# A written order for the first feed-forward block, a third raw buffer, and first attention tiles taken from three batches

## The chip, the cores and the metric

The kernel runs on one core of a Trainium2 chip. Its engines are TensorE (PE in the rows; PEld is its weight load), VectorE (DVE), ScalarE (ACT), GpSimd (POOL) and SyncE (SP, which only issues transfers here); 16 DMA engines move the data. The metric is device time in microseconds (us) of one execution, the median of several; lower is better.

## The reference

Three stages in a row, with 3072 tokens (4 batches of 768), 8 heads of 40, a model width of 320 and a hidden width of 2048.

```python
# attention: an mLSTM recurrence over t, per batch and head
m_new  = max(f[t] + m, i[t]);  f_stab = exp(f[t] + m - m_new);  i_stab = exp(i[t] - m_new)
C      = f_stab * C + i_stab * outer(v[t], k[t]);   n = f_stab * n + i_stab * k[t]
y[t]   = sigmoid(o[t]) * (C @ q[t]) / max(|n . q[t]|, 1)
# first feed-forward layer
h = maximum(x @ w_in, 0);  x = (h * h) @ w_out
# second feed-forward layer
h = x @ w2_in;  x = (h * sigmoid(h)) @ w2_out
```

## The kernel before, in words

**Gates.** The recurrence is computed in 24 tiles of 128 tokens, six chunks c for each batch b. `gate_math` runs two scans over all 768 steps on 32 partitions (batch times head) on VectorE, which give `gg` (a log weight) and `eg` (its exponent). Both are written to DRAM (`g_d`, `e_d`) so that transfers can read them back spread over 128 partitions. `gate_T` transposes two more rows into `aw`.

**An attention tile** i goes through small functions: `load_q` and `load_v` (tiles `kq`, `vk`), `load_w` (512 KB of `g_d` spread into `W`), `WT` (GpSimd masks `W`), `WE` (eight exponents on ScalarE), `SC` (scores, TensorE into `sc`), `SD` (VectorE, scores times `W`), `HG` (TensorE into `hA`: the tile's own part, and for c > 0 the earlier chunks' part from the state `cm`), `EV` (VectorE: division and output gate `sg`, into `y`), `ST`, `GR` (the new state), `XT`, `XA`, `XL` (transpose `y` and split it into a high and a low part in `x`). For c > 0, `QT` scales q by `eq`, which `load_e` reads back from `e_d`. The first six tiles use float32 matmuls, each of which the trace shows as two.

**The first layer** works on eight blocks of 384 tokens (three tiles). Hidden slice j of 16 takes eight matmuls into `hin` ("in j"), a Relu and two squares on ScalarE (`r`, `gh`, `r` again), a subtraction on VectorE (`gl`), and eight matmuls into `o` ("out j"). TensorE is three slices ahead with "in" (`AHEAD`). The second layer has six blocks of 512 tokens.

**Weights** arrive as 64-bit numbers, in 16 pieces per layer (eight "in", eight "out"). Each piece is loaded into a `raw` buffer (two of them), turned into float32 by one ScalarE (L171) and two VectorE instructions (L173, L174; tile `dt`), and split: ScalarE writes the high part (L185, L197), GpSimd the low one (L188, L189, L200 for the first layer). The first seven or so pieces are decoded before the first block begins, the others during it; the second layer's pieces follow during blocks 1 to 6 and go back to DRAM.

**Order.** Up to the first block a scheduler orders the engines, guided by the order of the code. From there TensorE's order is that of the code; in blocks 1 to 6 that of ScalarE, VectorE and SP too. Attention tiles 3 to 23 are spread over the blocks by `base` and `plan`. The first three tiles are (batch 0, chunk 0), (batch 1, chunk 0) and (batch 0, chunk 1), by

```python
TILES = [(b, c) for p in (0, 2) for c in range(NC) for b in (p, p + 1)]
```

Of the kernel before, what the change touches and what calls it, by code (L numbers as in the profile page):

```python
# [22 lines left out]
L = 128  # L23
# [8 lines left out]
EC = 1  # L32
W_BUFS = 2
N_NAT = 6
W_U0 = 4
# [4 lines left out]
G_PAT = "a"  # L40
W_LA = 4
TILES = [(b, c) for p in (0, 2) for c in range(NC) for b in (p, p + 1)]
# [19 lines left out]
def mlstm_moe_kernel(  # L62
# [39 lines left out]
    ident = const.tile([128, 128], F32, name="ident")  # L102
    bmask = const.tile([128, 9, 1], F32, name="bmask")
# [7 lines left out]
    gg = gp.tile([32, S], F32, name="gg")  # L111

# [4 lines left out]
    def consts():  # L117
        pool.memset(eg, 1.0)
        pool.memset(eg.rearrange("p (c t) -> p c t", t=L)[:, :, 0:1], 0.0)
        make_identity(nc, ident)  # L120
        pool.memset(bmask, 1.0)
# [7 lines left out]
    def gate_math():  # L129
        dve.tensor_tensor_scan(out=w_r, data0=fg, data1=a_r, initial=NEG, op0=ALU.add, op1=ALU.max)  # L130
        dve.tensor_tensor(out=fg[:, 1:S], in0=fg[:, 1:S], in1=w_r[:, 0:S - 1], op=ALU.add)
        dve.tensor_tensor(out=fg[:, 1:S], in0=fg[:, 1:S], in1=w_r[:, 1:S], op=ALU.subtract)
        dve.memset(fg[:, 0:1], 0.0)
        dve.tensor_tensor_scan(out=gg, data0=eg, data1=fg, initial=0.0, op0=ALU.mult, op1=ALU.add)
        act.activation(out=eg, in_=gg, func=ACTF.Exp)
        dve.tensor_tensor(out=a_r, in0=a_r, in1=w_r, op=ALU.subtract)
        dve.tensor_tensor(out=a_r, in0=a_r, in1=gg, op=ALU.subtract)
        g3 = gg.rearrange("p (c t) -> p c t", t=L)
        dve.tensor_tensor(out=w_r.rearrange("p (c t) -> p c t", t=L),
                          in0=a_r.rearrange("p (c t) -> p c t", t=L),  # L140
                          in1=g3[:, :, L - 1:L].to_broadcast([32, NC, L]), op=ALU.add)
        act.activation(out=w_r, in_=w_r, func=ACTF.Exp)
        sp.dma_start(out=g_d, in_=gg)
        sp.dma_start(out=e_d, in_=eg)

    def gate_T():
        ps = p_at.tile([128, 512], F32, tag="at", name="gT")
        pv = ps[:, 0:2 * NC * 32].rearrange("p (a c r) -> p a c r", a=2, r=32)
        for k, src in enumerate((a_r, w_r)):
            for c in range(NC):  # L150
                pe.transpose(pv[:, k, c, :], src[:, c * L:(c + 1) * L], ident[0:32, 0:32])
        dve.tensor_copy(out=aw, in_=pv)
# [4 lines left out]
    def w_in_load(w, u, pl):  # L157
        st = pl.tile([128, 3, 256, 2], I32, tag="raw", name="raw")
        sp.dma_start(out=st, in_=w[u].bitcast(I32).rearrange("p (k f two) -> p k f two", k=3, two=2))
        return st.rearrange("p k f two -> p (k f) two")  # L160

    def w_out_load(w, u, pl):
        st = pl.tile([128, 768, 2], I32, tag="raw", name="raw")[:, 0:640]
        sp.dma_start(out=st, in_=w[u].bitcast(I32).rearrange("p (n two) -> p n two", two=2))
        return st

    def w_split(raw, which, layer, u, pl):
        n = 768 if which == "i" else 640
        lo, hi = raw[:, :, 0], raw[:, :, 1]
        t = pl.tile([128, 768], I32, tag="dt", name="dt")[:, 0:n]  # L170
# [6 lines left out]
        if which == "i":  # L177
# [3 lines left out]
            else:  # L181
                ws = pl.tile([128, 1280], F32R, tag="raw", name="ws")
# [4 lines left out]
            eng = pool if layer == 1 else dve  # L187
            eng.tensor_tensor(out=w[:, 3:5], in0=tv[:, 0:2], in1=f(w[:, 0:2]), op=ALU.subtract)  # L188
            eng.tensor_tensor(out=w[64:128, 2], in0=tv[64:128, 2], in1=f(w[64:128, 2]), op=ALU.subtract)  # L189
        elif layer == 1:  # L190
# [8 lines left out]
            for c, oh, ol in parts:  # L199
                pool.tensor_tensor(out=w[:, :, ol], in0=tv[:, :, c], in1=f(w[:, :, oh]), op=ALU.subtract)  # L200
        else:
            ws = pl.tile([128, 1280], F32R, tag="raw", name="ws")
# [18 lines left out]

    eq = [at.tile([128, 3, EC * L], F32, name=f"eq{k}") for k in range(2)]
    cc2 = [at.tile([128, H, 42], F32, name=f"cc{k}") for k in range(2)]
    T = {}

    def at_consts():
        for k in range(2):
            pool.memset(eq[k][:, 2, :], 0.0)
            pool.memset(cc2[k], 0.0)

    def load_q(i):
        b, c = TILES[i]
# [12 lines left out]
    def load_v(i):  # L245
        v = T[i]["vk"] = at.tile([128, DM + 2 * VW], F32, tag="vk", name="vk", bufs=2)
# [15 lines left out]
    def load_w(i):  # L262
        b, c = TILES[i]
        d = T[i]
        w = at.tile([128, H, L], F32, tag="W", name="W", bufs=W_BUFS)
        d["W", 0], d["W", 1] = w[:, 0:4], w[:, 4:8]
        sp.dma_start(out=w, in_=g_d[b * H:(b + 1) * H, c * L:(c + 1) * L].unsqueeze(0).to_broadcast([128, H, L]))

    def load_e(i):
        b, c = TILES[i]  # L270
        if c % EC == 0 and c + EC > 1:
            for g in range(3):
                n = min(3, H - 3 * g)
                h = b * H + 3 * g
                sp.dma_start(out=eq[b % 2][0:40 * n, g, :],
# [556 lines left out]
```

## Time and profile before

| | |
|---|---|
| median of 3 runs | 872.77 us (871.34 to 873.82) |
| profiled execution | 871.93 us, its span 869.9 us |
| TensorE busy | 832.7 us, 96% of the span |
| weight loads busy | 784.0 us, 90% |
| VectorE, ScalarE | 493.1 and 495.5 us, 57% each |
| GpSimd | 97.3 us, 11% |
| transfers | 117.41 MB, 135 GB/s over the span |

The span runs from the first to the last instruction. Matmuls are pipelined, so each one's time in the trace is longer than the distance to the next; the pace of TensorE is read from start to start. An average over the span hides that the stages have different limits, so most views below are of single stretches.

### The profile page before, as it was taken

The numbers are of one execution on the slowest core, as the hardware profiler recorded it, in microseconds if no ns is written. First come the engines' busy times: TensorE is split into PE (matmuls) and PEld (weight loads), VectorE is DVE, ScalarE is ACT, GpSimd is POOL, SyncE is SP. The second block draws the span as 40 slices with busy tenths as digits, with TensorE's granted clock in tenths as the row PEclk, the third lists the DMA queues.
The fourth block names the chain that finished last, engine by engine and source line by source line (L and its number), as shares of the span: only waits on it lengthen the run. The fifth ranks groups of instructions, "written<-read, shape, count | busy, mean of one in ns | idle before, by whom it ended". The sixth has DMA issues, their size and how long they took to land.

```text
span 869.9 us, 14594 instructions
## 1 busy us (share of the span) xinstructions
PE 832.7 (96%) x5492; PEld 784.0 (90%) x5492; DVE 493.1 (57%) x879; ACT 495.5 (57%) x969; POOL 97.3 (11%) x119
## 2 busy tenths in 40 slices
PE   4768989999999999999999999999999999999998
PEld 3758989999999999999999899999999999999997
DVE  5466756777778778787852234353343443533432
ACT  4567846787797777977855563343343433433332
POOL 4574500000101000100000010000000000000000
PEclk9999999999999999999999999999999999999999
DMA  8786455767767768768510894020020000000000
GB/s 241 236 277 188 130 165 181 237 212 220 234 212 228 245 189 246 234 218 255 171 57 31 256 293 153 1 80 1 1 79 1 1 31 1 31 1 1 31 0 31
DMA packets 71391, 117.41 MB, mean 135 GB/s; under 512 B 5146, under 2 KB 50138, under 8 KB 71082
## 3 DMA queue, kind: packets, MB, share of 16 engines
q1 hardware_dynamic: 71322, 116.49, 43.0%
q8 instruction: 43, 0.70, 0.3%
q14 instruction: 26, 0.21, 0.1%
HBM read 77.23 MB, written 19.33 MB: 111 GB/s over the span
## 4 chain that ended last, share of the span: by engine, by line
PE 76%; DMA 8%; DVE 5%; ACT 5%; SPq 2%; issue 2%; POOL 1%; DVEq 0%; ACTq 0%; POOLq 0%
PE hin L539 36%; PE o L594 6%; PE o L593 6%; PE o L592 6%; PE o L575 4%; PE o L577 4%; PE o L576 4%; DMA eq<-e_d 3%; PE hA L406 2%; PE o L580 2%; PE o L582 2%; DMA raw<-in_w_in_dram 2%; DMA sg<-in_og_dram 1%; PE sc L331 1%; PE hA L396 1%
## 5 line engine op out<-in xcount | busy, mean ns | idle before, releaser
L539 PE MATMUL hin<-x,wi 128*128 128x384 f32 (+1 forms) x1792 | 401.9, 366 | 7.7 <-ACT r L547 4.5
L539 PEld LDWEIGHTS hin<-x,wi 128*128 128x128 f32 x1792 | 324.2, 190 | 36.4 <-ACT r L547 5.8
L559 DVE TENSOR_TENSOR gl<-r,gh 128x384 fp32r<-128x384 f32 (+1 forms) x224 | 142.7, 639 | 113.8 <-ACT gh L556 60.7
L555 DVE TENSOR_TENSOR r<-hin,r 128x512 f32<-128x512 f32 x96 | 66.4, 691 | 136.4 <-ACT r L554 136.4
L554 ACT ACTIVATE r<-hin 128x512 f32<-128x512 f32 x96 | 57.3, 597 | 148.2 <-PE hin L539 148.2
L594 PE MATMUL o<-wo,gl 128*128 128x320 f32 x384 | 118.7, 309 | 0.0
L593 PE MATMUL o<-wo,gh 128*128 128x320 f32 x384 | 118.5, 309 | 0.0
L592 PE MATMUL o<-wo,gh 128*128 128x320 f32 x384 | 118.2, 308 | 0.0
L547 ACT ACTIVATE r<-hin 128x384 f32<-128x384 f32 x128 | 62.3, 486 | 79.2 <-PE hin L539 72.4
L556 ACT ACTIVATE gh<-r 128x512 fp32r<-128x512 f32 x96 | 60.6, 632 | 65.4 <-DVE r L555 65.4
L575 PE MATMUL o<-gh,wo 128*128 128x384 f32 x256 | 90.2, 352 | 0.0
L577 PE MATMUL o<-gl,wo 128*128 128x384 f32 x256 | 86.7, 339 | 0.0
L576 PE MATMUL o<-gh,wo 128*128 128x384 f32 x256 | 86.6, 338 | 0.0
L592 PEld LDWEIGHTS o<-wo,gh 128*128 128x128 f32 x384 | 72.1, 188 | 3.6
L593 PEld LDWEIGHTS o<-wo,gh 128*128 128x128 f32 x384 | 72.1, 188 | 3.6
L308 POOL TENSOR_SCALAR_AFFINE_SELECT W<-W 128x512 f32<-128x512 f32 x48 | 39.2, 841 | 301.1 <-DMA W<-g_d 189.6
L594 PEld LDWEIGHTS o<-wo,gl 128*128 128x128 f32 x384 | 72.1, 188 | 0.0
L316 ACT ACTIVATE W<-W,aw 128x128 f32<-128x128 f32 x192 | 59.9, 388 | 16.8 <-POOL W L308 16.7
L548 ACT ACTIVATE gh<-r 128x384 fp32r<-128x384 f32 x128 | 67.2, 525 | 3.8
L550 ACT ACTIVATE r<-r 128x384 f32<-128x384 f32 x128 | 67.0, 524 | 3.7
L575 PEld LDWEIGHTS o<-gh,wo 128*128 128x128 f32 x256 | 48.5, 189 | 0.5
L576 PEld LDWEIGHTS o<-gh,wo 128*128 128x128 f32 x256 | 48.5, 189 | 0.1
(108 smaller groups left out, 1060.1 us busy)
## 6 DMA issues: line engine op xcount, KB each, us to landing
stk<-tt SPq DMA_DIRECT2D x162, 120.0 KB
raw<-in_w_in_dram SPq DMA_DIRECT2D x16, 768.0 KB
W<-g_d SPq DMA_DIRECT2D x24, 512.0 KB
raw<-in_w_out_dram SPq DMA_DIRECT2D x16, 640.0 KB
vk<-in_vk_dram SPq DMA_DIRECT2D x24, 328.0 KB
rqk<-in_qk_dram SPq DMA_DIRECT2D x18, 360.0 KB
w2i_d<-ws SPq DMA_DIRECT2D x8, 640.0 KB
w2o_d<-ws SPq DMA_DIRECT2D x8, 640.0 KB
```

Source lines behind the costliest of these rows:

```text
L539: pe.matmul(ps[:, 0:N], w[:, c, ws], x[:, sl, 0:N], start=(k == 0), stop=(k == 7))
L547: act.activation(out=r, in_=ps[:, 0:N], func=ACTF.Relu)
L548: act.activation(out=gh, in_=r, func=ACTF.Square)
L550: act.activation(out=g, in_=r, func=ACTF.Square)
L555: dve.tensor_tensor(out=g, in0=ps[:, 0:N], in1=r, op=ALU.mult)
L559: low.append(lambda: on("gl" if ly == 1 else "gl2", gi).tensor_tensor(out=gl, in0=g, in1=f(gh), op=ALU.subtract))
L575: pe.matmul(o[k][:, 0:N], w[:, c], gh, start=first, stop=False)
L576: pe.matmul(o[k][:, 0:N], w[:, c2], gh, start=False, stop=False)
L577: pe.matmul(o[k][:, 0:N], w[:, c], gl, start=False, stop=last)
L592: pe.matmul(o[k][:, 0:DM], gh[:, c], w[:, 0:320], start=first, stop=False)
L593: pe.matmul(o[k][:, 0:DM], gh[:, c], w[:, 320:640], start=False, stop=False)
L594: pe.matmul(o[k][:, 0:DM], gl[:, c], w[:, 0:320], start=False, stop=last)
```

## The change

Everything up to the end of the first block is no longer left to a scheduler. Each step gets a name, a planned time from a table (`ORDER`) and a list of steps that must stand ahead of it; all are sorted by that time and written out in that order on all five engines. Besides:

- the first three tiles are chunk 0 of batches 0, 1 and 2 (so none of them reads `cm` or `eq`), and batch 3 comes last, its six chunks one behind the other;
- the gate scans are cut into chunk 0 and the other five chunks; `g_d` of chunk 0 and `W` of tiles 0 to 2 are issued from ScalarE's queue;
- there are three `raw` buffers for two; "in" pieces are loaded ahead of "out" pieces (i0, i1, o0, i2, ...);
- the scores of the first six tiles have four heads on partitions 0 to 39 and four on 64 to 103, in turn;
- in the first block some squares move from ScalarE to VectorE, the low parts of pieces i1, i7, o3, o4 and o6 from GpSimd to VectorE;
- 21 filler matmuls of 512 columns on zeros (`warm`) stand between the first ones, two of them behind the start of the block.

```diff
+GA = L
+RAW_BUFS = 3
+DT_BUFS = 2
-TILES = [(b, c) for p in (0, 2) for c in range(NC) for b in (p, p + 1)]
+WARM = ((4, "o0"), (5, "o0"), (2, "in"), (3, "in"), (3, "in"), (2, "in"), (2, "in"))
+ORDER = """
+    gates 0 ee0 0 sg:0 0.05 q:0 0.1 q:1 0.2 c1 0.26 v:0 0.3 c0 0.39 c2 0.4 v:1 0.5 warm0 0.98 gD0 1.24 wz 1.62
...
+PLAN = {k: float(v) for k, v in zip(ORDER.split()[0::2], ORDER.split()[1::2])}
...
+TILES = [(b, c) for c in range(NC) for b in range(3)] + [(3, c) for c in range(NC)]
...
+            lambda: (act if first else sp).dma_start(out=g_d[:, c], in_=gg[:, c]),
+            lambda: sp.dma_start(out=e_d[:, c], in_=eg[:, c]),
...
+    def warm(n, tag="o2"):
+        ps = (p_in if tag == "in" else p_out).tile([128, 512], F32, tag=tag, name="warm")
+        for _ in range(n):
+            pe.matmul(ps.rearrange("p (h t) -> p h t", h=4), wz, wz.unsqueeze(1).to_broadcast([128, 4, L]),
+                      start=True, stop=True)
...
-            eng = pool if layer == 1 else dve
+            eng = pool if layer == 1 and PLAN.get(f"@Mi{u}", 1) else dve
...
+        q, m = (act, 4) if i < N_EARLY else (sp, H)
+        for p in range(0, H, m):
+            q.dma_start(out=w[:, p:p + m], in_=g_d[b * H + p:b * H + p + m, c * L:(c + 1) * L].unsqueeze(0).to_broadcast([128, m, L]))
...
+                for h in range(4):
+                    for p in range(2):
+                        x = d["kq"][64 * p:64 * p + D]
+                        pe.matmul(d["sc", p][:, h * L:(h + 1) * L], x[:, 0, h], x[:, 1, h], start=True, stop=True)
...
+            if bi == 0 and PLAN.get(f"@g{j}", j in ON_DVE):
+                dve.tensor_tensor(out=r, in0=r, in1=r, op=ALU.mult)
+            else:
+                act.activation(out=r, in_=r, func=ACTF.Square)
...
+        order_of = sorted(first, key=when)
...
+            order.enter_context(tc.manual_schedule(engines={e.engine for e in (pe, act, dve, pool, sp)}))
+            for n in order_of:
+                first[n][1]()
```

Before, SP issues `g_d`, and behind it, among other loads, the `W` tiles that read it back (here from the gate scan on):

```order
L143 DMA g_d<-gg 32x768
L236 DMA kq<-in_qkn_dram 40x2048
L144 DMA e_d<-eg 32x768
L267 DMA W<-g_d 128x8x128 x2
L159 DMA raw<-in_w_in_dram 128x1536
L275 DMA eq_111<-e_d 120x1x128 x2
L275 DMA eq_111<-e_d 80x1x128
L164 DMA raw<-in_w_out_dram 128x1280
L275 DMA eq_112<-e_d 120x1x128 x2
```

Of the change, ScalarE's own order from its start holds both (`x` is the borrowed buffer in which tile 2's `W` lies):

```order
L364 ACTIVATE sg<-sg 128x960
L207 ACT_TABLE_LOAD
L207 ACTIVATE eg<-gg 32x128
L213 DMA g_d<-gg 32x128
L212 ACTIVATE w_a<-w_a 32x128
L376 DMA W<-g_d 128x4x128 x4
L376 DMA x<-g_d 128x4x128 x2
L212 ACTIVATE w_r<-w_r 32x640
L207 ACTIVATE eg<-gg 32x640
L425 ACTIVATE W<-W,aw 128x128 x12
```

The `W` loads have moved from SP to ScalarE's queue, behind the first sigmoid and the first exponent, ahead of the other gate exponents and of the tiles' own exponents.

On VectorE before, at the place where the third tile's `x` is written (the second row here) and the first block begins, the next four weight pieces stand (names with numbers):

```order
L174 SCALAR_TENSOR_TENSOR dt_776<-raw_445,dt_776 128x768
L474 TENSOR_TENSOR x_258<-xT_456,x_258 128x3x128
L173 TENSOR_SCALAR dt_838<-dt_838 128x640
L174 SCALAR_TENSOR_TENSOR dt_838<-raw_774,dt_838 128x640
L173 TENSOR_SCALAR dt_906<-dt_906 128x768
L174 SCALAR_TENSOR_TENSOR dt_906<-raw_836,dt_906 128x768
L559 TENSOR_TENSOR gl_520<-r_521,gh_519 128x384
L173 TENSOR_SCALAR dt_958<-dt_958 128x640
L174 SCALAR_TENSOR_TENSOR dt_958<-raw_904,dt_958 128x640
L559 TENSOR_TENSOR gl_535<-r_536,gh_534 128x384
```

At the same place in the change (the third tile's `x` is the fourth row):

```order
L602 TENSOR_TENSOR x_396<-xT_427,x_396 128x3x128
L254 TENSOR_SCALAR dt_355<-dt_355 128x768
L255 SCALAR_TENSOR_TENSOR dt_355<-raw_208,dt_355 128x768
L602 TENSOR_TENSOR x_396<-xT_433,x_396 128x3x128
L269 TENSOR_TENSOR wi1_458<-dt_355,wi1_458 128x512
L270 TENSOR_TENSOR wi1_458<-dt_355,wi1_458 64x256
L670 TENSOR_TENSOR r_478<-r_478 128x384
L678 TENSOR_TENSOR gl_477<-r_478,gh_476 128x384
L462 TENSOR_TENSOR pn_509<-sc_499,W_306 128x512
L670 TENSOR_TENSOR r_494<-r_494 128x384
L678 TENSOR_TENSOR gl_493<-r_494,gh_492 128x384
L254 TENSOR_SCALAR dt_411<-dt_411 128x640
```

Only two pieces are decoded ahead of the block now (i0 and i1), 14 inside it, and between them stand squares (`r` from `r`) and a low part (`wi1`) that were not on VectorE.

## Rows read from the trace of the kernel before

**Rows 1.** Stretches: PE, PEld, DVE, ACT, POOL busy (instructions), granted clock, DMA share, GB/s

```profile
0.00:58.90 58.90, 35.14 (x150) 30.94 (x150) 34.74 (x56) 32.84 (x74) 35.38 (x53) 1.00 0.82 246
...
73.60:143.90 70.30, 66.55 (x455) 63.17 (x455) 44.90 (x91) 46.38 (x100) 21.87 (x23) 0.98 0.55 170
58.90:143.90 85.00, 77.60 (x486) 73.06 (x487) 52.33 (x101) 56.02 (x116) 28.48 (x31) 0.98 0.56 176
...
200.00:490.00 290.00, 289.54 (x2312) 284.06 (x2311) 206.98 (x411) 216.70 (x452) 21.55 (x26) 1.00 0.62 195
490.00:870.00 380.00, 374.64 (x2088) 341.26 (x2086) 153.97 (x221) 145.72 (x241) 7.99 (x6) 1.00 0.16 50
```

**Rows 2.** TensorE's timeline: start, us, engine, line, tiles, count [idle before, releaser]

```profile
58.89 0.69 PE L539 MATMUL hin<-x,wi 128*128 128x384 f32 x1 [0.89 <-ACT x L470]
60.40 5.17 PE L539 MATMUL hin<-x,wi 128*128 128x384 f32 x15 [0.82 <-DVE x L474]
...
76.17 1.56 PE L539 MATMUL hin<-x,wi 128*128 128x384 f32 x8
77.56 0.33 PE L575 MATMUL o<-gh,wo 128*128 128x384 f32 x1
...
82.86 1.16 PE L326 MATMUL sc<-kq 40*128 40x128 f32 x8
...
143.88 1.57 PE L539 MATMUL hin<-x,wi 128*128 128x384 f32 x8
```

**Rows 3.** Timeline of the start, all engines

```profile
3.53 1.80 DVE L130 TENSOR_TENSOR_SCAN w_r<-fg,a_r 32x768 f32<-32x768 f32 x1 [3.53 <-DMA a_r<-in_gates_dram]
...
8.34 1.00 ACT L260 ACTIVATE sg<-sg 128x960 f32<-128x960 f32 x1 [6.26 <-DMA sg<-in_og_dram]
9.36 1.28 ACT L135 ACT_TABLE_LOAD   x1
9.94 0.33 SPq L143 DMA_DIRECT2D g_d<-gg  x1
...
16.75 1.01 SPq L267 DMA_DIRECT2D W<-g_d  x2
...
32.67 0.16 DVE L412 TENSOR_SCALAR den<-hA 128x8 f32<-128x8 f32 x1
...
34.10 0.20 DVE L421 COPY y<-y 128x64 f32<-128x64 f32 x1
...
44.49 0.55 DVE L474 TENSOR_TENSOR x<-xT,x 128x384 fp32r<-128x384 f32 x1
```

**Rows 4.** Groups by line and form, 0 to 60 us: busy us, mean ns | idle before

```profile
L341 DVE TENSOR_TENSOR pn<-sc,W 128x512 f32<-128x512 f32 x7 | 4.8, 685 | 6.6 <-ACT W L316 6.4 <-issue 0.2
L316 ACT ACTIVATE W<-W,aw 128x128 f32<-128x128 f32 x40 | 12.3, 387 | 6.3 <-POOL W L308 6.3
L308 POOL TENSOR_SCALAR_AFFINE_SELECT W<-W 128x512 f32<-128x512 f32 x10 | 8.2, 843 | 0.5 <-DMA W<-g_d 0.3
```

**Rows 5.** The same view of VectorE, 58.9 to 143.9 us (the first block)

```profile
L559 DVE TENSOR_TENSOR gl<-r,gh 128x384 fp32r<-128x384 f32 x18 | 13.0, 735 | 7.5 <-ACT r L550 7.3
L174 DVE SCALAR_TENSOR_TENSOR dt<-raw,dt 128x768 int32<-128x768 int32 x5 | 4.9, 982 | 0.1
L174 DVE SCALAR_TENSOR_TENSOR dt<-raw,dt 128x640 int32<-128x640 int32 x4 | 4.2, 1040 | 0.1
L341 DVE TENSOR_TENSOR pn<-sc,W 128x512 f32<-128x512 f32 x6 | 4.1, 676 | 0.9 <-PE sc L326 0.9
...
L173 DVE TENSOR_SCALAR dt<-dt 128x768 int32<-128x768 int32 x4 | 3.4, 838 | 4.0 <-ACT dt L171 4.0
L173 DVE TENSOR_SCALAR dt<-dt 128x640 int32<-128x640 int32 x4 | 2.4, 604 | 8.2 <-ACT dt L171 8.2
```

**Rows 6.** TensorE in a gap and behind it: busy, granted clock, DMA share, GB/s

```profile
121.00:124.00 3.00, 0.98 (x6) 1.00 0.59 169
124.00:126.00 2.00, 1.07 (x5) 0.60 0.79 240
```

More of the change, by code (lines that the diff above doesn't have):

```diff
@@ L111, in mlstm_moe_kernel @@
     gg = gp.tile([32, S], F32, name="gg")
+    w_a = gp.tile([32, GA], F32, name="w_a")
     def load_gates():
@@ new lines, in plan @@
+            for nm, x, fn in todo:
+                if x < KF or f"{nm}:{i}" in PLAN:
+                    after = [f"{y}:{i}" for y in need.get(nm, "").split() if y not in ("gd",)]
+                    if nm in ("w", "e"):
+                        after += ["gD1", "eD1"]
+                    if nm in ("m0", "x0", "vk"):
+                        after += ["take"]
+                    if nm in ("sk", "sj") and i < N_NAT:
+                        continue
+                    if nm == "h" and TILES[i][1]:
+                        after.append(f"gm:{i - 3}")
+                    if nm == "gr" and TILES[i][1]:
+                        after += [f"gr:{i - 3}", f"h:{i}"]
+                    if nm == "gm" and TILES[i][1]:
+                        after += [f"h:{i}"]
+                    if nm == "ev":
+                        after.append(f"si:{i // 3 * 3}")
+                    after = [y for y in after if y != f"sj:{i}" or i >= N_NAT]
+                    GUESS[f"{nm}:{i}"] = F0 + SLOT * x
+                    add(f"{nm}:{i}", lambda fn=fn: fn(i), *after)
+                else:
+                    at_slot(x, lambda fn=fn: fn(i))
@@ L708, in run_events, with tr, take @@
                 fn()
+        g1, g2 = gate_parts(0, GA, w_a), gate_parts(GA, S, w_r[:, GA:S])
+        cp = {}
+        def tr(key, *a):
+            return lambda: cp.update({key: gate_T(*a)})
+        def take(key):
+            return lambda: cp.pop(key)()
+        add("gates", load_gates)
+        add("wz", lambda: dve.memset(wz, 0.0))
+        add("c0", consts)
+        add("c1", at_consts)
+        add("c2", consts2)
+        for k, (n, tag) in enumerate(WARM):
+            add(f"warm{k}", lambda n=n, tag=tag: warm(n, tag), "wz")
@@ L721, in mlstm_moe_kernel, with when @@
+        eff = {}
+        def when(n):
+            if n not in eff:
+                eff[n] = None
+                assert n in first, n
+                t, _, after = first[n]
+                eff[n] = max([t] + [when(a) + 1e-4 for a in after])
+            assert eff[n] is not None, n
+            return eff[n]
+        order_of = sorted(first, key=when)
         with ExitStack() as order:
+            order.enter_context(tc.manual_schedule(engines={e.engine for e in (pe, act, dve, pool, sp)}))
+            for n in order_of:
+                first[n][1]()
+            order.close()
```

464 lines of the change are left out of this document (302 added, 162 removed).

## The prediction

> **What bounds the kernel now.** I read the stretches first [rows 1], to see which engine is full where. From 200 us on TensorE never rests: 289.5 of 290 us, then 374.6 of 380, while VectorE and ScalarE are at most three quarters busy. Nothing that shortens their work there can shorten the kernel. Time is to be had only up to the end of the first block. TensorE's timeline [rows 2] gives two marks: its first "in" matmul at 58.89 us, and 143.88, where the last "out" of the first block has ended and the second block runs on. Before the first mark TensorE is busy 35.1 of 58.9 us, and on latency: it does three attention tiles in pieces, each waiting for another engine. Between the marks lie 85.0 us, of which 77.6 busy [rows 1]. Behind the second mark come 869.9 − 143.9 = 726 us with some 6 us of idle time (mostly the end), which no edit touches except through the order of the tiles.
>
> So the forecast is a sum of three terms: when the first "in" starts, how long the first block then takes, and whether the 726 us stay.
>
> The pace of TensorE is to be read from start to start. Eight "in" matmuls take 77.56 − 76.17 = 1.39 us in the middle of the block, 0.174 each; the first ones take 5.17 / 15 = 0.34 each [rows 2], twice that. The granted clock reads 1.00 in that first stretch, so the records do not show why; in 124 to 126 us they do: after 3 us in which TensorE was busy for 0.98, it reads 0.60, a mixture of the 2.4 and 1.2 GHz levels [rows 6].
>
> **Term 1, the start.** What is on the path in the changed kernel, step by step. The first scan starts at 3.53 as before [rows 3]. With 128 of 768 columns the two scans and four small steps need about a sixth of theirs; `gg` of chunk 0 is there at about 5, no longer at 9.9. But the transfer that writes it now stands on ScalarE's queue behind the first sigmoid, and that waits for `sg`. Before, `sg` is the fifth load and the sigmoid starts at 8.34. Now it is the third, right behind the gates (in by 3.5): 0.49 MB at 246 GB/s [rows 1] is 2 us, so 5.6. Sigmoid 1.00, table load 1.28 [rows 3], a short exponent 0.3: `g_d` is issued at 8.4.
>
> Before, it is issued at 9.94, and SP can issue `W` only at 16.75 [rows 3]: the 0.1 MB landed 6.8 us later, behind 3.8 MB of loads already in the same queue. On ScalarE's queue nothing is ahead of it. Bounds: a landing 2 us after the issue (the gates take about that) or behind the whole backlog (a rival, below). I take 2.5: `W` from 10.9 on. Three `W` tiles are 1.57 MB; SP still has 2.6 MB of its 4.9 MB outstanding by then, so I give `W` half of 246 GB/s, 4.3 us a tile: 15.2, 19.4 and 23.7. GpSimd's mask adds 0.84 to the first half [rows 4], and ScalarE's exponents follow at 12.3 / 40 = 0.31 each: the third tile's eight end at 27.0. (The first two tiles' exponents, and weight steps of 0.9 and 0.8, fit between 16.8 and 24.6.)
>
> Behind that VectorE's order decides, as it is full: the last product (0.69 [rows 4]), a copy (0.3), `EV` of the second tile (32.67 to 34.30, 1.63), `XL` 0.55, `EV` of the third 1.63, `XL` 0.55 [rows 3], piece i1 (0.84 + 0.98 [rows 5]), `XL` 0.55: 7.7 us, so 34.7. With hand-overs I take 36. The range is 33 (`W` lands faster) to 41 (it lands behind everything). The filler matmuls, 21 of 512 columns at an estimated 0.23 to 0.46 each (512 / 384 of the two paces above), lie in TensorE's waits and cost nothing there; if they did lie on the path, the 5 in front of the last transposes and the block would be 1 to 2 us. Term 1: 36 − 58.9 = **−22.9**.
>
> What the new tile order removes here: the third tile before is chunk 1, needs `eq` and `cm`, and is the reason for a part of the 58.9. Its work does not vanish, it moves into the block (tile 3).
>
> **Term 2, the first block.** TensorE first. From 73.6 to 143.9 it is busy 66.55 of 70.3 [rows 1], with 16 "out", but only 15 "in", since four came before, and all of tiles 3 to 5 but half of one tile's scores. In the change all 19 "in" (the first three slices of block 1 among them) come after the mark: 66.6 + 4 × 1.39 + 1.1 (half a tile's scores [rows 2]) = 73.2. Two things may lower it. The spell at the lower clock is in the 66.6, about 2 us. And the scores of tiles 3 to 5, 3 × 2.2 = 6.5 us, now alternate between partitions 0 and 64: if such pairs overlap, 3.3 less; if not, nothing. No row shows a pair. So the floor is 68 to 73; I take 70.
>
> VectorE next, the engine that gains work. Before, it is busy 52.3 us between the marks [rows 1], with four "in" and four "out" pieces. Now 14 pieces fall in the block: four more "out" at 0.604 + 1.040 and two more "in" at 0.838 + 0.982 [rows 5], 10.2. Nine squares of 128x384, at the price of `gl`, which has that shape (0.735): 6.6. Five low parts from GpSimd, each a subtraction of 512 columns (0.676, the product `L341`, is the nearest row) and a smaller one: 1.1 and 5.5. Less: one tile's `EV` and state steps, two `gl`, one second-layer piece that fall outside now, about 8. Together 66 to 67 us, against 70 for TensorE.
>
> ScalarE loses 11 squares and two Relu-square pairs and gains seven piece steps; from 56.0 [rows 1] it stays below 56.
>
> So two engines, each full for 66 to 70 us, follow one fixed order. What they add to the larger is waiting. Before, TensorE is idle for 7.4 of 85.0. The likely places now are known: "out 0" needs piece o0, whose VectorE step stands two squares, two `gl`, one product and the low part of i1 behind the last `XL` (about 43), then ScalarE, behind the next tiles' sigmoid and table load, then GpSimd, 2 us: about 46, where TensorE has done three or four "in" and the scores of tile 3 by 44. SP is held for that too: its `sg` load of the second block waits for the last read of the first `sg` at about 33, and behind it stand o1's raw load and tile 4's `W`; both are wanted from 45 on. The third raw buffer lets a load run two pieces ahead, so the chain from one decode to the load that needs its buffer (0.4 + some 4 us) hides under the 9 to 11 us of VectorE work that lie between a decode and the third one behind it. I take 5 us of waits on top of 70: 75, within 68 (none, pairs overlap) and 85 (as now). Term 2: 75 − 85.0 = **−10.0**.
>
> **Term 3, the rest.** The last six tiles are one batch, one chunk behind the other. The state of a tile is planned 4.9 slices after its scores start, and wanted by the next at 5.3 + 3.3 = 8.6. At 726 us for 13 blocks of 16 slices, 3.5 a slice, that is 13 us of room. **0**, ±1.
>
> **Sum.** −22.9 − 10.0 = −32.9 on a span of 869.9: 837.0. The profiled execution took 871.93, the median of the runs is 872.77, 0.8 above it; 872.8 − 32.9 = **840**.
>
> **Rivals.**
> (A) The sum itself, start 33 to 39, block 71 to 79: 833 to 847, chance 0.62.
> (B) The order fits: TensorE does not wait, pairs overlap. 34 + 68 = 102, so 42 us less: 831. For it speaks that TensorE is at 66.6 of 70.3 already now in this stretch; against it, that VectorE has 15 us more to do. 0.12.
> (C) The queues are no help: `g_d` lands behind SP's backlog, 4.9 MB at 246 GB/s, at 22, and three `W` tiles then take 6.4 at the full rate: 28.4 for 23.7, 5 us later, 845. For it speaks the 6.8 us of before; against it, that this was one queue. 0.10. The Trainium skill ("DMA: Bandwidth & Descriptors", section "Issuing engines are not separate DMA queues") says that starting transfers from several engines saves only the sequencer's issue time. No run here has two queues yet to agree or not.
> (D) VectorE and GpSimd hold each other up. GpSimd works 28.5 us of the 85 now [rows 1]; with the tiles' masks and states it comes to about 36 in 75. If each of those stopped VectorE for two thirds of its time, VectorE would need 66 + 24 = 90, and the mark would fall at 36 + 92: 857. For it: nowhere before is GpSimd this busy beside a full VectorE. Against: where GpSimd is busy for 60% (35.4 of 58.9 [rows 1]), the product `L341` takes 0.685 [rows 4], no more than the 0.676 of the block [rows 5]. 0.13. The Trainium skill ("SBUF — State Buffer", section "SBUF: two separate sides") describes a port pair that the two share by an exclusive lock, which a VectorE instruction with two SBUF inputs takes against a GpSimd one that reads SBUF; `L341` has one operand in PSUM and would be spared, the decode's second step would not.
> (E) Slower: the serial batch. Place: tiles 18 to 23, in blocks 5 to 7. Each of five hand-overs would have to be 32.9 / 5 = 6.6 us late for the gain to be gone, beyond the 13 us of room. 0.03: over 873.
>
> **How the numbers follow.** The likeliest case is A at 840. The range of 829 to 855 takes in A, B and C and leaves out most of D, and E. This measurement can tell about 0.3%, 2.6 us. Faster: A, B, C and D, 0.96. Slower: E, 0.03. The same: 0.01, a D and a slow start together.
>
> **What would show it.** Right: the first `hin` at 33 to 39; its matmuls 0.174 apart from the first on; the "out" of block 1 beginning within 71 to 79 us of it; VectorE over 85% busy in that block; the remaining stretch 726 ± 2. Wrong in term 1: `W` issued after 12 or the masks waiting for `W` until 26 or later. Wrong in term 2: TensorE waiting for `gl` or a weight's low part by more than 10 us in total, or under 2. D shows as longer VectorE rows, above all the decode's second step.

## The result, and the profile after

The changed kernel takes 857.11 us (median of 4, 855.78 to 857.24); the kernel before took 872.06 beside it (870.83 to 873.82). The ratio is 0.9824, 95% interval 0.9802 to 0.9845: faster by about 15 us or 1.8%, where 32.9 us were forecast.

The stretches of the profiled execution of after, cut at the same two marks; columns as in [rows 1]:

```profile
0.00:44.80 44.80, 32.39 (x149) 24.90 (x149) 25.59 (x51) 19.75 (x49) 17.39 (x35) 1.00 0.75 224
44.80:130.90 86.10, 75.59 (x499) 69.39 (x499) 74.67 (x124) 65.44 (x133) 39.81 (x37) 0.96 0.65 205
200.00:490.00 290.00, 288.95 (x2268) 284.05 (x2268) 201.33 (x403) 213.61 (x441) 21.24 (x25) 1.00 0.65 201
130.90:855.50 724.60, 720.15 (x4869) 681.34 (x4868) 409.22 (x732) 406.17 (x781) 39.02 (x41) 1.00 0.40 124
```

The first "in" starts at 44.79, not 58.89; the second mark lies at 130.9, not 143.88. So the three terms of the forecast came out as −14.1 (forecast −22.9), +1.1 (−10.0) and −1.4 (0): 86.1 − 85.0 for the block, 724.6 − 726.0 for the rest. They add up to the difference of the spans, 855.5 − 869.9 = −14.4. All but 0.3 us of the gain is an earlier start; the block, which was to get 10 us shorter, gets 1.1 us longer. VectorE goes from 52.3 to 74.7 us in it, GpSimd from 28.5 to 39.8, and ScalarE, which was to stay below 56, from 56.0 to 65.4.

ScalarE in the start (timeline; start us, us, engine, line, count [idle before, releaser]):

```profile
5.37 1.00 ACT L364 ACTIVATE sg<-sg 128x960 f32<-128x960 f32 x1 [3.28 <-DMA sg<-in_og_dram]
5.38 0.35 ACTq L213 DMA_DIRECT2D g_d<-gg  x1
...
9.85 3.34 ACTq L376 DMA_DIRECT2D W<-g_d  x4
...
21.55 0.73 ACT L212 ACTIVATE w_r<-w_r 32x640 f32<-32x640 f32 x1 [13.37 <-DVE w_r L210]
...
22.82 3.60 ACT L425 ACTIVATE W<-W,aw 128x128 f32<-128x128 f32 x12
...
29.60 2.43 ACT L425 ACTIVATE x<-x,aw 128x128 f32<-128x128 f32 x8
```

`g_d` is issued at 5.38, beside the first sigmoid and ahead of the table load and not behind them, three us sooner than the forecast had it, and the first `W` at 9.85 (10.9 there). But then ScalarE stands for 13.37 us at the exponent of the late gate chunks, which needs VectorE's scan of them. VectorE goes on with that scan only at 14.38, behind a copy that waits for a transpose, and on TensorE 30 matmuls of scores (9.68 to 14.0) stand ahead of this transpose. Tile 0's exponents start at 22.82, and the third tile's end at 29.60 + 2.43 = 32.0 (27.0 in the forecast).

TensorE in the same stretch, same view:

```profile
26.13 5.35 PE L523 MATMUL hA<-vk,W 128*128 128x42 f32 x24
...
33.70 1.49 PE L232 MATMUL warm<-wz 128*128 128x512 bf16 x3
34.97 0.85 PE L588 MATMUL xT<-ident,y 128*128 128x128 f32 x3
35.61 3.48 PE L523 MATMUL hA<-x 128*128 128x42 f32 x16
38.89 1.49 PE L232 MATMUL warm<-wz 128*128 128x512 bf16 x3
40.17 0.85 PE L588 MATMUL xT<-ident,y 128*128 128x128 f32 x3
42.21 0.88 PE L588 MATMUL xT<-ident,y 128*128 128x128 f32 x3 [1.20 <-DVE y L542]
42.88 1.06 PE L232 MATMUL warm<-wz 128*128 128x512 bf16 x2
...
44.79 4.08 PE L647 MATMUL hin<-x,wi 128*128 128x384 f32 x16
```

Two sets of filler matmuls (`warm`) stand directly in front of the transposes of tiles 0 and 1, 1.28 us each from start to start, and a third of two in front of the states, 0.85 us. From the last exponent to the first "in" it is 12.8 us; the forecast had 9.0. The chain that ends last does not go through that exponent: it leaves VectorE with tile 0's first product of scores and `W` at 24.9, and from there to 41.0 TensorE has no gap at all (16.07 us busy, VectorE 10.5).

TensorE's waits between the marks (engine, line, releaser: us in total, times, longest):

```profile
PE hin L647 <- POOL wi L269: 2.6, 2, 1.9
PE o L704 <- DVE gl L678: 1.5, 1, 1.5
PE warm L232 <- ACT r L657: 1.4, 1, 1.4
PE hin L647 <- DVE x L602: 1.3, 1, 1.3
PE o L703 <- DVE wo L281: 1.2, 1, 1.2
PE hin L647 <- ACT r L657: 1.1, 1, 1.1
PE o L703 <- POOL wo L281: 0.6, 1, 0.6
```

No wait is long, and three other engines' work stands in the list. Idle time is 86.10 − 75.59 = 10.5 us. Two of the waits, the 1.5 us for `gl` and the 1.9 us for `wi`, have a slower pace behind them:

```profile
65.00:67.50 2.50, 0.96 (x6) 0.64 (x6) 2.40 (x7) 2.49 (x7) 0.19 (x1) 1.00 0.73 179
67.50:71.80 4.30, 4.30 (x20) 4.21 (x19) 4.20 (x8) 2.21 (x7) 2.13 (x2) 0.60 0.61 196
...
77.80:80.00 2.20, 0.43 (x3) 0.11 (x1) 1.85 (x4) 1.99 (x6) 2.20 (x2) 1.00 1.02 392
80.00:84.40 4.40, 4.32 (x16) 4.05 (x17) 3.92 (x7) 4.00 (x11) 1.73 (x3) 0.64 0.88 288
```

In 65.0 to 67.5 TensorE is busy for 0.96 us; in the 4.3 us behind that the granted clock reads 0.60, a mixture of the 2.4 and the 1.2 GHz levels. The same at 77.8, and 0.64 behind it. Behind the other long one, the 1.4 us in front of `warm` at 54.35, it reads 1.00. The two spells cost 0.40 × 4.3 + 0.36 × 4.4 = 3.3 us, and the first 16 "in" take 4.08 for 16 × 0.174 = 2.8. So of the 75.6 us busy some 71 are TensorE's work at full pace.

### The profile page after: what moved, and what is told of

Read it like the earlier page. It is cut to its first block, busy times and chain, and to the rows that moved or that the text cites. A ratio compares the mean times of both kernels' runs of the same rounds, so it can differ in the third digit from the quotient of the medians.

```text
span 855.5 us, 14574 instructions
## 1 busy us (share of the span) xinstructions
PE 828.1 (97%) x5513; PEld 775.6 (91%) x5513; DVE 509.5 (60%) x907; ACT 491.4 (57%) x962; POOL 96.2 (11%) x113
## 4 chain that ended last, share of the span: by engine, by line
PE 88%; DMA 3%; DVE 3%; POOL 2%; SPq 1%; ACT 1%; issue 1%; POOLq 0%; DVEq 0%
PE hin L647 39%; PE o L721 7%; PE o L720 7%; PE o L719 7%; PE o L702 5%; PE o L703 5%; PE o L704 5%; PE hA L528 3%; PE o L707 2%; PE o L709 2%; PE hA L517 2%; PE sc L449 2%; PE hA L523 1%; PE st L555 1%; PE xT L588 1%; DMA raw<-in_w_in_dram 1%
## 5 line engine op out<-in xcount | busy, mean ns | idle before, releaser
L647 PEld LDWEIGHTS hin<-x,wi 128*128 128x128 f32 x1792 | 320.6, 189 | 34.6 <-POOL wi L269 3.7
L678 DVE TENSOR_TENSOR gl<-r,gh 128x384 fp32r<-128x384 f32 (+1 forms) x224 | 139.8, 626 | 108.9 <-ACT gh L664 60.7
L664 ACT ACTIVATE gh<-r 128x384 fp32r<-128x384 f32 (+1 forms) x224 | 127.9, 571 | 69.2 <-DVE r L660 65.4
L660 DVE TENSOR_TENSOR r<-hin,r 128x512 f32<-128x512 f32 x96 | 66.3, 691 | 136.4 <-ACT r L659 136.4
L417 POOL TENSOR_SCALAR_AFFINE_SELECT W<-W 128x512 f32<-128x512 f32 x46 | 41.2, 916 | 249.2 <-ACT gh L664 84.1
L672 ACT ACTIVATE r<-r 128x384 f32<-128x384 f32 x119 | 62.4, 525 | 3.6
L425 ACT ACTIVATE W<-W,aw 128x128 f32<-128x128 f32 x184 | 57.7, 388 | 0.3 <-POOL W L417 0.2
L704 PEld LDWEIGHTS o<-gl,wo 128*128 128x128 f32 x256 | 48.6, 190 | 2.2 <-DVE gl L678 2.2
```

The costliest lines, as they stand in the source:

```text
L647: pe.matmul(ps[:, 0:N], w[:, c, ws], x[:, sl, 0:N], start=(k == 0), stop=(k == 7))
L660: dve.tensor_tensor(out=r, in0=ps, in1=r, op=ALU.mult)
L664: act.activation(out=gh, in_=r, func=ACTF.Square if blocks[bi][0] == 1 else ACTF.Copy)
L672: act.activation(out=r, in_=r, func=ACTF.Square)
L678: on("gl" if ly == 1 else "gl2", gi).tensor_tensor(out=gl, in0=r, in1=f(gh), op=ALU.subtract)
L704: pe.matmul(o[k][:, 0:N], w[:, c], gl, start=False, stop=last)
```

## The experiments

Times of each run, read from its own trace: the first "in"; the block from there to the second mark; busy time of VectorE, GpSimd and ScalarE in the block; the median of its runs. The kernels that leave the block as it is in after (after itself, the first two, W on SP, four raw buffers) have 85.6 to 86.5, but each block is read from one execution, and the executions of one kernel lie 1.0 to 5.6 us apart; so a difference of 1 to 3 us is weak, and is read with the medians. In the run with ScalarE's squares out the traced execution, 854.2 us, is the slowest of four (the others 848.6 to 850.9). The stretch behind the block is 722.4 to 727.7 in all runs; medians that differ by 2 us tell little.

| run | first "in" | block | VectorE | GpSimd | ScalarE | median |
|---|---|---|---|---|---|---|
| after | 44.8 | 86.1 | 74.7 | 39.8 | 65.4 | 857.1 |
| no fillers | 41.0 | 86.4 | 75.1 | 40.4 | 66.3 | 855.1 |
| exponents first | 41.5 | 85.6 | 75.5 | 40.2 | 65.4 | 854.7 |
| W on SP | 44.0 | 86.5 | 74.5 | 40.1 | 65.4 | 856.8 |
| no squares | 45.0 | 83.3 | 68.6 | 38.7 | 65.3 | 855.8 |
| squares on ScalarE | 44.0 | 84.8 | 69.0 | 38.2 | 69.3 | 854.3 |
| GpSimd writes only | 42.6 | 86.0 | 66.3 | 44.5 | 65.5 | 855.4 |
| GpSimd short | 45.0 | 81.3 | 65.7 | 29.2 | 65.1 | 851.5 |
| six trades of place | 44.0 | 90.0 | 75.2 | 40.1 | 65.4 | 861.0 |
| two raw buffers | 45.3 | 99.8 | 72.5 | 37.1 | 65.3 | 873.3 |
| four raw buffers | 45.0 | 85.8 | 76.6 | 40.4 | 65.4 | 857.6 |
| GpSimd short, no squares | 45.2 | 78.0 | 60.8 | 30.1 | 64.9 | 849.6 |
| that, ScalarE's squares out | 45.7 | 81.0 | 61.8 | 29.9 | 61.6 | 850.3 |
| three edits | 40.4 | 84.9 | 69.5 | 38.3 | 70.0 | 852.2 |
| all edits | 39.4 | 86.6 | 68.3 | 38.9 | 69.9 | 854.5 |
| three edits, four raw | 40.3 | 83.1 | 71.2 | 39.2 | 69.9 | 850.0 |

**The start: fillers.**

```
-WARM = ((4, "o0"), (5, "o0"), (2, "in"), (3, "in"), (3, "in"), (2, "in"), (2, "in"))
+WARM = ()
```

> The 21 filler matmuls are left out; the order of all else stays. In the changed kernel the first 'in' starts at 44.79 us and the block's end (the mark) lies at 131.3. Theory P (fillers stand on the path: in front of the last pieces of attention and of the transposes, 0.9 + 1.3 + 1.3 us): the first 'in' comes about 3 us earlier, at 41.5 to 42.5, and the mark moves with it unless its first matmuls get slower. Rival Q (they pay for themselves: they keep the clock up for the block): the first 'in' comes earlier by the same 3 us or by nothing, but its first 32 matmuls go 0.34 apart as in the kernel before, not 0.19 to 0.26, which costs 3 to 4 us, so that the mark stays within 1 us or comes later.

TensorE at the place shown above, in this run:

```profile
33.30 0.88 PE L588 MATMUL xT<-ident,y 128*128 128x128 f32 x3
33.97 3.48 PE L523 MATMUL hA<-x 128*128 128x42 f32 x16
37.25 0.88 PE L588 MATMUL xT<-ident,y 128*128 128x128 f32 x3
```

Now the third tile's products stand directly behind the first transposes, and the second transposes behind these. The first "in" is 3.7 us earlier, about the 3.4 of the three sets, and the mark 3.4. Theory P: the fillers were on the path. What Q says is there too, but small: from the first "in" to the third slice's it takes 5.9 us without fillers (41.05 to 46.91) and 5.1 with them (44.79 to 49.89).

**The start: tile 0's exponents first** (two entries of the table).

```
-we1 11.91    ee1 12.24
+we1 15.7     ee1 15.71
```

> On ScalarE the eight exponents of tile 0 are put in front of the two exponents of gate chunks 1 to 5, which wait for VectorE until 21.55 us; nothing else moves. Theory H (ScalarE's order: tile 0's masked W lies ready from 18.5 on behind that wait): the tile's exponents run from about 18.5 to 21.5, ScalarE is 2.5 us ahead from 23 on, the last exponent of the third tile ends at 29.5 to 30.5 and not at 32.0, and the first 'in' starts at 42 to 43.5 and not at 44.79. Rival W (the landing of the W tiles and their masks set the start): the last exponent ends at 31.5 or later, the first 'in' at 44 or later. For the block: if VectorE is full from the start on (theory V), the mark moves by less than half of what the first 'in' moves; if the block's length is its own (rival L), the mark moves by the same.

ScalarE in this run:

```profile
19.30 2.45 ACT L425 ACTIVATE W<-W,aw 128x128 f32<-128x128 f32 x8 [11.16 <-POOL W L417]
22.32 0.73 ACT L212 ACTIVATE w_r<-w_r 32x640 f32<-32x640 f32 x1 [0.56 <-DVE w_r L210]
...
28.55 2.43 ACT L425 ACTIVATE x<-x,aw 128x128 f32<-128x128 f32 x8
```

The eight exponents of tile 0 run at 19.30, while the gate chunks are not there yet, and the third tile's end at 31.0. The first "in" moves by 3.3 us, 0.5 more than theory H allowed, and the mark by 3.8; the block keeps its length. So theory H holds for the direction, but not for the way: the last exponent moves by only 1.0 us, since ScalarE now waits 0.96 us for VectorE's decode of piece i0 and splits that piece ahead of the third tile's exponents. Most of the gain lies on TensorE, whose first 24 products `hA` go at twice the pace:

```profile
24.62 2.87 PE L523 MATMUL hA<-vk,W 128*128 128x42 f32 x24
```

From their start to the next instruction they take 2.70 us, and 5.14 in after. The granted clock reads 1.00 in both stretches, so the rows do not show why. VectorE is not the bound from the start on, or the mark would have stayed.

**The start: the queue.**

```
-lambda: (act if first else sp).dma_start(out=g_d[:, c], in_=gg[:, c]),
+lambda: (sp if first else sp).dma_start(out=g_d[:, c], in_=gg[:, c]),
-q, m = (act, 4) if i < N_EARLY else (sp, H)
+q, m = (sp, 4) if i < N_EARLY else (sp, H)
```

> g_d of chunk 0 and the first three W tiles are issued by SP again, not by ScalarE, at their places in the table (behind the first two keys and values). In the changed kernel g_d is issued at 5.38, W from 9.85 on, and the last half of tile 1's W is there at 24.5. Theory Q (another engine's queue is what lets them pass the loads): W is issued at 14 or later, and the first 'in' comes 3 us or more later than 44.8. Theory C (the queue makes no difference, the bytes ahead and the rate do): W is issued within 2 us of 9.85 and the first 'in' starts within 1.5 us of 44.8.

SP's queue in this run:

```profile
6.76 0.35 SPq L213 DMA_DIRECT2D g_d<-gg  x1
...
11.99 0.93 SPq L376 DMA_DIRECT2D W<-g_d  x2
```

`W` is issued 2.1 us later than from ScalarE, and the first "in" comes at 44.0, not later. From the issue of `g_d` to that of `W` it takes 5.2 us here and 4.5 in after; the forecast had 2.5 for it. Theory C, but for 0.1 us in `W`'s issue: which engine issues them decides nothing here. That is what the Trainium skill says ("DMA: Bandwidth & Descriptors", section "Issuing engines are not separate DMA queues"), and this run agrees. Since tile 0's masked `W` lies ready at 20.0 in after, 2.8 us before its exponents, the run does not show what 2 us would do where `W`'s landing is on the path.

**The block: VectorE's squares**, left out and moved.

```
 if bi == 0 and PLAN.get(f"@g{j}", j in ON_DVE):
-    dve.tensor_tensor(out=r, in0=r, in1=r, op=ALU.mult)
+    pass                      # no squares
...
-if bi == 0 and PLAN.get(f"@g{j}", j in ON_DVE):
+if False:                     # squares on ScalarE
```

> The nine squares of the first block that VectorE does are left out altogether (those slices use the Relu's output in their low part, which is timing only): 6.0 us of VectorE's 75.1 go, nothing is added elsewhere. Theory V (VectorE's amount of work sets the block's length): the block, 86.5 us from the first 'in' to the mark, gets 4 to 6 us shorter, and the run about 851 to 853 us. Rival L (single late hand-overs and the slow pace behind them set it, with slack on VectorE between): less than 2 us, run 855 to 857.

> The same nine squares go back to ScalarE, as in the kernel before: VectorE loses 6.0 us and ScalarE gains 9 x 0.523 = 4.7 us, 70.3 in a block of 86.5. Theory V: the block gets 3 to 6 us shorter, since ScalarE has 20 us to spare. Rival L: within 1 us. Rival S (ScalarE is late too, since its Relus and exponents then stand behind more): 1 to 4 us longer.

2.8 us for 6.0 us of VectorE's work, and 1.3 when ScalarE does it instead: between the theories, and the first run's median, 855.8, lies where theory L had it (1.4 us below after's). VectorE's amount of work counts for less than half its price, and is not alone.

**The block: GpSimd beside VectorE.** In the first run GpSimd's low part is a subtraction of 8 columns and three writes of a constant; in the second there is one write.

```
-eng.tensor_tensor(out=w[:, 3:5], in0=tv[:, 0:2], in1=f(w[:, 0:2]), op=ALU.subtract)
+pool.tensor_tensor(out=w[:, 3, 0:8], in0=tv[:, 0, 0:8], in1=f(w[:, 0, 0:8]), op=ALU.subtract)
+for _ in range(3):            # 1 in the second run
+    pool.memset(f(w[:, 3:5]), 0.0)
...
```

> GpSimd's ten low parts of the first block (23.9 us of its 39.8) keep their place, their wait and about their length, but each is a subtraction of 8 columns and then three writes of a constant over the tile, which read nothing; the low parts are so left out, timing only. Theory D (VectorE and GpSimd hold each other up): rows of VectorE that lie beside such a subtraction were about twice as long (gl 1.54 and 0.87 for 0.56, the decode's second step 1.91, 1.77 and 1.52 for 0.96 and 0.82, y 1.61 for 0.49); they go back, VectorE's sum in the block falls from 75 to 64 to 67, and the block from 86.1 to 78 to 82. Rival N (the long rows are not due to GpSimd's reading, or they lie in VectorE's slack): VectorE's sum stays within 2 us of 75, or the block within 2 of 86.

> As the run before it, but with one write of the constant in place of three, so that each low part is short besides (some 0.6 us in place of 2.4; the low parts are left out, timing only). Theory G (GpSimd's own length is on the path: at 53.8 to 65.2 us of the changed kernel the chain runs through one GpSimd instruction after another): the block is 2 to 5 us shorter than in the run before it. Rival (only the holding up counts): within 1 us of the run before it.

What the question is about, in the timeline of after (GpSimd and VectorE):

```profile
86.19 1.51 POOL L269 TENSOR_TENSOR wi<-dt,wi 128x512 fp32r<-128x512 f32 x1 [4.31 <-ACT wi L266]
86.61 1.77 DVE L255 SCALAR_TENSOR_TENSOR dt<-raw,dt 128x640 int32<-128x640 int32 x1
87.78 1.20 POOL L270 TENSOR_TENSOR wi<-dt,wi 64x256 fp32r<-64x256 f32 x1
88.31 1.09 DVE L670 TENSOR_TENSOR r<-r 128x384 f32<-128x384 f32 x1
```

While GpSimd subtracts, the decode's second step (0.82 elsewhere in this form) takes 1.77 and the square 1.09 (0.55 elsewhere). VectorE's groups in the block of after (mean ns of one behind the sum), as in [rows 5]:

```profile
L678 DVE TENSOR_TENSOR gl<-r,gh 128x384 fp32r<-128x384 f32 x17 | 11.2, 669 | 0.6 <-ACT r L672 0.4
L255 DVE SCALAR_TENSOR_TENSOR dt<-raw,dt 128x640 int32<-128x640 int32 x8 | 8.2, 1031 | 0.3
L255 DVE SCALAR_TENSOR_TENSOR dt<-raw,dt 128x768 int32<-128x768 int32 x7 | 8.1, 1156 | 0.2
```

and in the run in which GpSimd only writes:

```profile
L690 DVE TENSOR_TENSOR gl<-r,gh 128x384 fp32r<-128x384 f32 x17 | 10.3, 616 | 2.8 <-ACT r L684 2.6
L255 DVE SCALAR_TENSOR_TENSOR dt<-raw,dt 128x768 int32<-128x768 int32 x7 | 7.1, 1016 | 0.2
L255 DVE SCALAR_TENSOR_TENSOR dt<-raw,dt 128x640 int32<-128x640 int32 x8 | 6.6, 825 | 0.3
```

The decode's second step goes from 1031 to 825 and from 1156 to 1016 ns, and VectorE's sum from 74.7 to 66.3 us. So GpSimd's reading does hold VectorE up, by 8.3 us in this block. The Trainium skill ("SBUF — State Buffer", section "SBUF: two separate sides") describes the lock on the port pair that the two share; the run agrees with it. But the block does not get shorter by that: GpSimd is busy 44.5 us here (three writes take longer than the subtraction), and TensorE's waits on its low parts go from 3.2 to 5.2 us. With one write it is 81.3, 4.7 less than with three, as theory G had it, and the median goes from 855.4 to 851.5:

```profile
45.00:126.30 81.30, 72.11 (x500) 66.75 (x500) 65.75 (x125) 65.11 (x133) 29.22 (x52) 1.00 0.70 216
```

VectorE free and GpSimd short give 4.8 us together; VectorE free and GpSimd as long as before gave nothing. No run has GpSimd short and VectorE held up, so whether VectorE's 8.3 us have any part in the 4.8 is not shown.

**The block: the order.** Six entries of the table (these alone are shown) trade places with their neighbours.

```
-si:3 31.53  gl2 37.34  m0:5 44.14  sk:6 53.68  M14 66.55  d0:6 69.59
+si:3 34.0   gl2 36.2   m0:5 45.5   sk:6 55.2   M14 64.95  d0:6 71.1
```

> Six instructions of the first block trade places with their neighbours in the table; no work is added or taken. Each is one behind which the row of a TensorE wait stood: tile 5's mask goes behind the low part of i4 (wait 1.9), the second sigmoid with its table load behind the next three ScalarE steps of weights (waits 1.4 and 0.6), the copies of tile 6's q and k behind the next Relu (1.1), the correction gl of slice 2 ahead of a decode (1.5), the low part of o6 ahead of a tile's output (1.2), tile 5's x split ahead of tile 6's products (1.3): 9.0 of the 10.5 us that TensorE is idle in the block. Theory L (single late hand-overs in a fixed order make up the block's excess, and each costs its wait and a slow stretch behind it): the block gets 4 to 9 us shorter than 86.1 and the run 847 to 852. Rival M (behind all of them stands one slower chain, the loads that SP issues when a buffer comes free and their landings of 4 to 7 us, so that other waits take their place): the block stays within 2 us.

The opposite of theory L: the block is 3.9 us longer. TensorE's longest waits in this run:

```profile
PE o L704 <- DVE gl L678: 3.1, 1, 3.1
PE st L555 <- DVE y L541: 2.9, 1, 2.9
PE hin L647 <- POOL wi L269: 2.2, 2, 1.2
```

The wait for `x` is gone, but one for `gl` is 3.1 us (1.5 in after), and a tile's states wait 2.9 us for the product `y`, 0.3 in after. Other hand-overs become late in place of those that were moved; which of the six trades does it was not taken apart.

**The block: raw buffers.**

```
-RAW_BUFS = 3
+RAW_BUFS = 2
```

> Two raw buffers in place of three, all else as in the changed kernel. Rival M (loads that wait for a buffer are the chain behind the block): with one buffer less each load waits for a decode earlier, and the block gets 5 us or more longer. Theory L: 0 to 3 us longer, as the loads have slack.

SP's waits for VectorE's decode, which frees a raw buffer, in after between 25 and 131 us:

```profile
SPq L240 <- DVE dt L255: 13.5, 4, 6.0
SPq L245 <- DVE dt L255: 11.2, 4, 4.5
```

and with two buffers, between 25 and 145:

```profile
SPq L245 <- DVE dt L255: 32.6, 5, 16.2
SPq L240 <- DVE dt L255: 31.7, 6, 10.4
```

24.7 us become 64.3, and the block 99.8. The run as a whole takes 873.3 us, a ratio of 1.0028 (1.0008 to 1.0047) to the kernel before: with this table and without the third buffer nothing would have been gained. A fourth:

```
-st = pl.tile([128, 768, 2], I32, tag="raw", name="raw", bufs=RAW_BUFS)[:, 0:640]
+st = pl.tile([128, 640, 2], I32, tag="rawo", name="raw", bufs=2)    # RAW_BUFS = 2 for the "in" pieces
-v3 = at.tile([128, VW], BF16, tag="v3", name="v3", bufs=2)
+v3 = at.tile([128, VW], BF16, tag="v3", name="v3", bufs=1)
```

> Two raw buffers for the in pieces and two of their own for the out pieces, four in place of three (5 KB a partition more for the weights, made room for by one v3 buffer in place of two); the order is that of the changed kernel on every engine. Theory M (a load waits for a decode to free its buffer, and what stands behind it on SP's queue, W, q and k, waits too): SP's waits for the decode, 24.7 us between 25 and 131 us, fall below 12, and the block gets 4 to 9 us shorter than 86.1. Rival O (three buffers are enough; the one order of all engines, with TensorE, VectorE and GpSimd each waiting in turn, sets the block): SP waits less but the block stays within 2 us.

SP waits 14.2 us for the decode in place of 24.7, and the block is 85.8: rival O, though the waits did not fall below 12 as theory M's test wanted. Three are enough for this order.

**The block: several loads cut together** (the short GpSimd writes with the squares left out; then ScalarE's squares too).

> The short GpSimd low parts (left out, one write of a constant each) and no squares on VectorE (left out) together; timing only. VectorE comes to some 60 us in the block, GpSimd to 29, ScalarE stays at 65. Theory K (several loads together): more than the sum of the two alone, 4.8 + 2.8, so the block is 74 to 78 us. Rival O (chains through the order): the sum or less, 78.5 to 81.

> As the run before it, and ScalarE's nine squares of the block are left out too (4.6 us of its 65). Theory K: 72 to 76 us. Rival O: within 1 us of the run before it.

```profile
45.20:123.20 78.00, 71.18 (x499) 67.43 (x499) 60.83 (x116) 64.87 (x133) 30.09 (x52) 0.98 0.73 225
```

With VectorE at 60.8 us and GpSimd at 30.1 the block is 78.0: 8.1 shorter, where the two alone gave 4.8 + 2.8 = 7.6. They add, as far as single executions tell; that lies at the border of the two theories and decides for neither. With less work on ScalarE the block of the traced execution is 81.0, but that execution is 3.8 us above its kernel's median; the medians, 849.6 and 850.3, lie within rival O's 1 us, and the 72 to 76 of theory K are not there.

**Combinations.** No fillers, exponents first, squares on ScalarE:

> No fillers, tile 0's exponents in front of the late gate exponents, and the squares back on ScalarE, the three edits that moved the mark by 3.4, 3.8 and 2.2 us alone. If they add: first 'in' at 38 to 39, mark at 121.5 to 123, run 846 to 849 us. If the first two take away the same wait: first 'in' at 40 to 41, mark at 124 to 126, run 849 to 852.

First "in" at 40.4, 852.2 us: the first two, 3.7 and 3.3 us alone, give 4.4 together. That they take away the same wait is not the whole of it: the products `hA` go 0.21 us apart here, as in after, and not 0.11 as with the exponents first alone, so the gain in pace is gone. With the six trades of place and `vk:1 13.6, vk:0 13.7` besides:

> The three edits of the combined run, the six hand-overs, and the weighting of tile 0's and 1's keys on GpSimd put behind tile 0's masks. By theory L the gains add: first 'in' at 38.5 to 40.5, a block of 76 to 82, run 841 to 847 us. By rival M: first 'in' the same, block 84 to 86, run 850 to 853.

39.4, the earliest start, but a block of 86.6, 1.7 us longer than without the trades. The three edits with four raw buffers:

> The same four raw buffers with the three edits of the combined run (no fillers, tile 0's exponents first, squares on ScalarE; first 'in' at 40.4 there, block 84.9). Theory M: first 'in' at 40 to 41, a block of 76 to 81, run 842 to 848 us. Rival O: block 83 to 86, run 850 to 853.

850.0 us (847.6 to 850.6), ratio 0.9758 (0.9740 to 0.9776): faster than both kernels, since this interval lies below that of after. Against the three edits alone (0.9753 to 0.9817) it can't be told apart.

## Why the prediction came out wrong, point by point

**Where the time is** was read rightly: behind the second mark nothing moved but 1.4 us, which is within the spread of that stretch over the runs, and the order of the last six tiles cost nothing that shows.

**Term 1** was mis-sized by 8.8 us, and two of its steps failed. The first is "Behind that VectorE's order decides, as it is full". TensorE decides: from 24.9 to 41.0 it has no gap, while VectorE is busy for 10.5 of these 16.07 us, and this work of TensorE stood in no term of the sum. With it fell that the fillers "lie in TensorE's waits and cost nothing there": 3.7 us, where the forecast had 1 to 2 if they lay on the path. Without them the tail from the last exponent (32.3 in that run) to the first "in" (41.05) is 8.7 us, next to the 9.0 of the forecast, but that is luck: there too the chain comes to the transposes through TensorE's products `hA` and not through VectorE's steps.

The second is "the third tile's eight end at 27.0": 32.0. Tile 2's masks end at 26.7 and not at 24.5, as GpSimd waits for tile 1's `W` until 24.46; and the working let the first tiles' exponents and the weight steps "fit between 16.8 and 24.6", without the exponent of the late gate chunks and without asking what these wait for: both that exponent and the split of piece i0 stand ahead of the third tile's exponents on ScalarE and wait for VectorE. Taking tile 0's exponents out from behind the first gave 3.3 us of start, 2.4 of them by TensorE's pace, and 1.0 at the last exponent. With both edits, and the squares moved, the last exponent still ends at 31.9 and the first "in" follows 8.5 us later, at 40.4: what is left of the 8.8 lies ahead of the last exponent. How much of it is `W`'s landing and how much ScalarE's order was not separated.

The forecast also had `g_d` issued at 8.4 and landed 2.5 us later; it was issued at 5.38 and took 4.5, two errors that nearly cancel. The sum let `W` pass SP's loads on ScalarE's queue and counted 5 us for it (the step from A to C); the run on SP shows that it is worth nothing here.

**Term 2** was mis-sized by 11.1 us, and the step that failed is "I take 5 us of waits on top of 70". TensorE's own 70 was right (some 71 measured); the pairs of scores overlap, 16 matmuls in 1.16 us where 8 took that before [rows 2]. VectorE's own 66 to 67 was right as a sum: 66.3 once GpSimd's low parts don't read beside it. ScalarE's "stays below 56" was wrong: 65.4. But TensorE waits 10.5 us, and loses some 4.6 more to the slow pace behind the waits and at the start (3.3 + 1.3 above), which the forecast had not added. What makes the waits is shown in part: VectorE's and GpSimd's load, with the 8.3 us that GpSimd's reading adds to VectorE's rows, is worth 8.1 of the 16 us over 70. What the other 8 hang on stays open. A fourth raw buffer and leaving out ScalarE's squares did not shorten the block. That the fixed order makes the waits is argued and not shown: six trades of place made it 3.9 us longer, so the order counts, but no run has an order planned afresh. "The third raw buffer lets a load run two pieces ahead" was right and is the largest single effect found, 13.7 us; the forecast gave it no number, since it was inside the 75.

**The rivals.** D gave 857, the time that was measured, but not by its sum: it had the start at 36 and the block at 92, and GpSimd's hold on VectorE at 24 us. Its mechanism is there, at 8.3 us, a fifth of GpSimd's 39.8 rather than two thirds, and the late start made the rest, so that the number was met by luck. What the prediction had named as its sign, longer rows of the decode's second step, is there (1156 for 982 ns [rows 5], the other form nearly unchanged, 1031 for 1040). Of C the headline holds, that the queues are no help, but not its sum: it had `g_d` land at 22, and `W`, which waits for that, was issued at 9.85 from ScalarE and at 11.99 from SP. B and E did not come.

**The signs.** The "in" matmuls were to go 0.174 apart from the first on; the first 16 took 4.08 us. "TensorE waiting for `gl` or a weight's low part by more than 10 us in total" was the sign against term 2; those are 5.9 (1.5 + 2.6 + 1.2 + 0.6), so the sign was set too narrow: the waits are spread over three other engines' work. And `W` was issued at 9.85, well before the 12 that was to speak against term 1, which was wrong all the same. Two signs of being right came: VectorE is 87% busy in the block, and the remaining stretch is 724.6.

## What to carry to other kernels

Before a stage is dated from the landing of its data, list what stands ahead of it on each in-order engine on the way, TensorE and its fillers too; here both steps that failed in the start were of that kind. Where three engines are each 75 to 90% full in one fixed order, don't add a fixed allowance of waits to the fullest: cutting VectorE's load gave less than half its price, and two of the late hand-overs also cost a slower pace behind them. Count buffers before order: in this order one raw buffer less cost 13.7 us and one more gave nothing.

## What the runs showed of the hardware that was not expected

VectorE instructions that lie beside a GpSimd subtraction of two SBUF operands took up to three times their time (decode 1.77 for 0.82 us, the product `y` 1.61 for 0.49); beside GpSimd writes of a constant the decode's second step did not (825 and 1016 ns on average). Two waits of 1.5 and 1.9 us on TensorE were followed by 4.3 and 4.4 us at a granted clock of 0.60 and 0.64, after stretches in which it was busy for 0.96 of 2.5 us and 0.43 of 2.2; behind one of 1.4 us it read 1.00. The same 24 matmuls went 0.214 and 0.112 us apart in two runs, both at a granted clock that reads 1.00.
